# VectorE turns y in 32 by 32 blocks of channel pairs, and the queries run over 32 rows on eight tiles of TensorE

## The chip, the cores and the metric

The kernel runs on one core of one Trainium2 chip. The metric is device time in microseconds (us); the kernel before takes 170.29 us, the median of three runs (170.18 to 171.32). A core has a matrix engine, TensorE (in the profile PE, with its weight loads as PEld), and VectorE (DVE), ScalarE (ACT), GpSimd (POOL) and SyncE (SP). GpSimd and SyncE do little here but issue DMAs, each from a queue of its own. TensorE writes to PSUM, eight banks of 512 float32 columns on 128 partitions; VectorE and ScalarE take its results from there (here: drain a bank).

## What is computed

The input x is 8 batches of 4224 tokens of 192 channels. First comes a convolution over the last 7 tokens, with softmaxed taps, one set for each group of 24 channels; call its result y. Then a token mixer without softmax:

```python
wq, wk = y @ w_q, y @ w_k                    # 192 -> 64
W_tok  = scale * einsum('bsd,btd->bst', wq, wk)
mixed  = einsum('bst,btd->bsd', W_tok, y)
out    = maximum(mixed, 0.0) @ w_out         # 192 -> 192
```

Both kernels use that mixed = wq @ (scale * w_k.T @ (y.T @ y)). So per batch they make y, the Gram matrix y.T @ y (192 x 192), the small matrix M (64 x 192) from it, the queries wq, mixed = wq @ M, its relu, and the product with w_out.

## The kernel before

A batch is cut into 35 chunks of 122 tokens (128 rows of x with the 6 ahead of them). **Loads** (L513) go out from GpSimd's queue and turn float32 into bfloat16 on the way; all eight batches have room in SBUF (tile xw), 18 chunks to a DMA, 9 in the first batch. **Convolution** (L315 to L317): a band matrix of 128 by 128 for each of 8 heads times 18 chunks of 24 channels; y then stands with tokens on partitions, and one drain (L621) copies two heads. **Transposes**: the Gram matrix (L744) takes y as it stands, but the queries need channels on partitions, so TensorE transposes the first 128 channels of each chunk (L321, or L322 and L323) and the other 64 of chunks in pairs (L678), and VectorE copies both out of PSUM (ytl L648, yth L688). **Queries** (L707, L711): 64 outputs for 512 tokens on each half of the array's columns, drained at L728. **M**: a small chain after the Gram matrix (L763, L807). **Mix** (L836, L848 or L856), then relu (L873 on ScalarE, L874 on VectorE) into rt. **Product** with w_out (L902 and L920), 192 columns each, two of four token classes to a drain (L941), and a store from SyncE's queue (L949), from four buffers of out_sb. The last 128 tokens of a batch have a block of their own.

**Shapes on TensorE.** An instruction may use the whole array (128*128 in the profile), half its columns (128*64) or half its rows (64*128). Two that use different halves run side by side. The PLAN says for each step with a choice which it is: F for the whole array, P for halves.

**Order.** Nothing is decided at run time. PLAN lists 960 steps with their engine and, for TensorE, the PSUM banks; each engine's instructions follow in that order, and a step waits by semaphores for what it needs and for its banks to be drained. The second half of a batch (mix, product) is interleaved with the first half of the next.

Of the kernel before, what the change touches and what calls it, by code (L numbers as in the profile page):

```python
# [6 lines left out]
ALU = mybir.AluOpType  # L7
# [5 lines left out]

PLAN = """
1D 38G 2D 13G 37G 39G 40G 8D 19D 41G 42G 9D 56G 57G 14D 58G 59G 60G 61G 62G 63G 5D 64G 15P 65G 12D 66G 67G
68G 69G 70G 71G 72G 73G 74G 0S 22D 75G 20D 76G 77G 78G 23D 24D 25A 16P6 6D 79G 80G 21D 11D 81G 26D 27D 17P
4D 28D 18A 29D 30P5 7D 33P6 34D 35D 31A 32A 36P 84F4 85D 90F3 91A 88P1 89D 86P5 87A 116P5 142P 94P2 95D 92F1
93A 96F3 43S 98F6 99A 97D 118F4 117D 106F5 102F1 104F3 82G 100F6 143P 107D 144P 3D 105A 103A 101D 145P 83G
110F5 108F6 109A 112F3 113A 111D 119D 114F0 120F1 115A 126P2 127D 130P6 131D 47A 124F0 48A 125D 46A 44S
122F5 128P2 146P 10D 147P 121D 49A 140P4 53A 50A 132P0 123D 138P3 129D 134P2 141D 148A 149P6 52A 133A 159P4  # L20
157P0 150D 45S 51A 151F6 135A 139D 160A 155F2 158D 161F4 154A 153A 152A 222P6 136P0 162A 137A 211P1 156D
171P4 197P 54A 224A 167P2 168A 213D 165P5 172D 169P0 198P 170A 166D 221P3 210P5 163P0 199P 55A 173F2 223D
225P3 212A 217P5 164A 214P0 226P 174D 179F2 218F 180D 219D 215F 227A 177F2 178D 244F4 175F3 216A 220S 181P5
264P0 233P6 202P 176D 243P2 246A 265A 182D 228P4 232P0 245A 235D 229P 254P6 256A 201P 234A 262P2 230D 231S
185P6 186D 263A 268P4 266P0 267A 200P 255P6 269D 195P3 187P2 196A 203D 239P4 236P0 257D 258P6 240F 188A 241A
183P3 184D 204F2 205A 237F 259F 247P4 250P2 248F 251F 238A 242S 260D 261S 249A 270F0 271A 189P6 190A 304P
276P4 277A 274P0 206P6 252D 253S 272P2 305P 191P4 208A 207A 209A 328P5 275D 273A 317P0 192D 330A 288P2 289D
290P3 278P4 279D 193P5 194D 318F6 329F2 319A 286F0 340F1 280F4 320A 321P5 331A 291D 332P2 287D 342A 335P0
322P 323A 281D 333P 336P 337A 309P 292P4 284F5 334D 338S 324P2 339P0 361P6 363A 325F 293D 282F4 341A 351P6
285D 298P5 353A 326D 327S 373P0 371P2 283D 306P 374A 302P4 303A 294P6 295A 375P0 299D 372D 300P5 301D 369P2  # L30
296P4 297D 362P6 307P 376A 343P0 350P4 370A 346P2 344P 364A 385F6 347F 352A 345D 308P 310D 357P0 348A 349S
365P4 354P2 358P 386D 311F5 312D 355F 356D 359A 360S 387F6 388D 313F5 316A 315A 366F 377F0 383F2 314A 447P5
411P 425P6 378A 384D 379P0 380D 367A 368S 449A 381P3 427A 436P2 438D 412P 424P5 435P0 382A 397P3 395P4 398D
389F2 426A 428P5 396D 431P3 437A 429P 432P 458P0 390D 430A 414P 460A 457P1 459A 442P5 433D 434S 439P3 415P
440F 441A 443F 444D 445S 446P1 468P0 413P 476P3 482P5 470A 448A 399P0 393P1 416P 469P2 483A 417A 477D 400D
478F3 453P5 471A 479A 394D 450P0 418F2 419D 454F 455A 451F 480F3 391F2 409P5 452A 456S 481D 401P6 402A 464P0
461P3 465P 466A 472P6 462P 392D 403P2 410D 463D 467S 492P5 493D 488P0 489A 518P 490P3 404D 407P5 491A 484P0
408D 485D 405P2 486P3 487A 406D 520P 494P5 495D 420P1 421A 423A 506P0 504P2 502P3 422A 531P4 505D 473F 554F1
496F2 507D 543F0 474D 475S 503D 533A 497D 532F6 500F5 556A 519P 516P2 542P3 545A 534D 535P0 501D 538P5 536F
537A 517D 539F 565F2 567A 544D 546P3 549P0 547P 550P 575P2 577A 540D 541S 548D 585P5 508P2 551A 552S 564P3  # L40
586D 553P0 555A 509D 523P 587P5 588A 522P 589P0 590A 566D 521P 576P6 583P4 578A 560P2 557P0 524D 525F6 526D
561F 558F 527F6 584A 562A 498F5 530A 579P4 559D 563S 528A 571P2 568P0 572P 580P 529A 573A 569P 499D 514P5
515A 512P6 513A 570D 574S 591P2 593P0 594A 581D 582S 639P5 510P4 599P6 592D 511D 600D 638P2 640A 595P0 601P4
602D 596A 641A 625P 597P2 650P6 652A 627P 660P0 642P4 661F6 598D 607F2 605F3 606D 662A 608D 643P 644D 663A
649P0 651A 626P 609P6 645P2 656P0 653P4 610D 646P 647D 648S 657P 654P 682P6 655D 684D 630P 658A 659S 628P
694P2 695A 613P0 603P1 683P6 690P4 691A 696P2 614D 611P0 629P 685A 604D 623P1 697A 692P4 693A 672P6 612D
617P0 615P3 624D 674D 671P1 618A 664P5 686P4 631D 632F0 616D 673A 665F 666A 706F3 633D 634F0 637A 687P 688A
689S 675P1 667P5 635A 707D 678P3 676P 636A 668P 669D 670S 679P 757P0 759D 732P 677A 702P1 700P5 680A 681S
701D 746P3 748A 619P0 620D 734P 756P3 758D 703A 745P5 733P 698P0 621P2 708P3 709D 747A 704P5 699A 622A 768P4
760P0 705A 752P2 761P 762A 770D 749P5 753P 710F4 711D 750F 779F1 781D 714P0 715D 754A 736P 720P2 763P3 778P0  # L50
751A 755S 767P5 780A 721D 764P 789P2 737P 791D 769D 735P 801P0 716P2 765A 766S 730P3 797P5 738D 718P4 731D
717D 790P3 802A 739P0 719D 712P1 713D 722P2 723D 798A 792A 740A 799P5 800A 803P3 771P0 793P2 772P 773A 774P5
804D 775P 782P3 776A 777S 785P0 783P 794P 795D 796S 786P 805P5 839P 784A 726P2 809P3 806D 787A 788S 811P0
810A 727D 724P5 813P6 814D 812A 807P3 728P2 815P0 816D 808A 725A 741P1 742A 821P6 822D 825P3 826D 823P4 744A
743A 853P1 729A 864P0 866A 852P5 854A 863P2 824D 855D 840P 875P0 877A 841P 827P4 859P5 865D 867P2 856P0 868P
860P 869A 857P 828D 886P4 861D 842P 870P2 874P5 858A 862S 876A 871P 896P0 897P1 888D 843P 817P4 885P5 872D
873S 878P2 898A 899A 881P0 879P 818D 837P4 838D 844P 887A 880A 819P6 829P5 845D 846P2 847A 892P3 820D 882P
900P6 893P 830D 831P2 848P5 883A 884S 833P0 832A 851A 901P 849A 894D 889P1 850A 904P4 906A 890P 905P3 907A
834D 917P0 902D 903S 835P6 891D 895S 928P4 930A 919D 908P2 916P0 909P 910A 911S 836D 929F6 931A 912P4 918D
913P 924P0 914A 915S 920P2 925P 926A 927S 941F6 943D 921F 932P4 953P0 955D 952P6 933P 922A 923S 940P2 942A  # L60
936P0 954D 937P 956P6 957P 934D 935S 944P2 945F 948P4 949P 938A 939S 958D 959S 946A 947S 950A 951S
""".split()

COL2, ROW2, FULL = "128x64", "64x128", "128x128"


class Op:


    n = 0  # L70

    def __init__(self, engines, emit, ns, needs=(), after=(), banks=0, drains=None, vt=0.0, mode=COL2, tail=0.0, whole=False):
        self.engines = (engines,) if isinstance(engines, str) else tuple(engines)
        self.emit = emit

        self.ns = ns

        self.needs = [x for x in needs if x is not None]

        self.after = [x for x in after if x is not None]  # L80
        self.banks = banks

        self.drains = drains
        self.vt = vt
        self.mode = mode

        self.whole = whole
        self.tail = tail
        self.users = 0
        self.bank = None  # L90
        self.engine = None
        self.end = None

        self.lands = 0.0

        self.size = 0
        Op.n += 1
        self.id = Op.n


class Planner:

    ENGINES = {"P": "PE", "F": "PE", "A": "ACT", "D": "DVE", "G": "POOL", "S": "SP"}

    def __init__(self, nbank):
        self.ops = []
        self.order = []
        self.nbank = nbank
# [8 lines left out]
    def plan(self):  # L117
        drains = {}
        for op in self.ops:
            if op.drains is not None:  # L120
                drains.setdefault(op.drains.number, []).append(op)
        users = [[] for _ in range(self.nbank)]
        place = {}
        for turn in PLAN:
            number, engine, bank = re.fullmatch(r"(\d+)([PFADGS])(\d*)", turn).groups()
            op = self.ops[int(number)]
            op.engine = self.ENGINES[engine]
            if engine == "F":
                assert op.whole
                op.mode = FULL  # L130
            assert op.engine in op.engines and op.number not in place
            if op.banks:
                op.bank = int(bank)
                for i in range(op.bank, op.bank + op.banks):
                    op.needs += users[i]
                    users[i] = drains[op.number]
            assert all(x.number in place for x in op.needs + op.after)
            place[op.number] = len(self.order)
            self.order.append(op)
# [892 lines left out]
```

## Time and profile before

| what | value |
|---|---|
| time, median of three runs | 170.29 us |
| the profiled execution: span from its first to its last instruction | 168.6 us |
| TensorE busy | 158.3 us, 94% |
| ScalarE busy | 123.8 us, 73% |
| VectorE busy | 116.2 us, 69% |
| granted TensorE clock | 0.994 |
| moved by DMA | 40.31 MB |

The page gives the profiled execution by its span; the median of the runs lies 1.7 us above that, and this is taken as what lies around the span. Busy time is the time in which at least one instruction of the engine is under way. In a line of the page, L744 is the line of the kernel, then come the engine, the operation, output and inputs, for TensorE the part of the array (rows*columns), the shape, how many, the busy time and the mean in ns; behind the second bar stands the idle time ahead of it and what ended it. A timeline row has the start in us, how long the row's instructions last together, and what they are. Matmuls overlap, so how fast they follow one another is read from the starts of neighbouring rows, not from the duration of one.

### The profile page before, as it was taken

The page shows a single profiled execution, that of the slowest core. Times are in us where ns is not written, and L with a number is a line of the kernel's source. Part 1 is how long each engine was busy: PE and PEld are TensorE (multiplying, and loading weights), DVE is VectorE, ACT ScalarE, POOL GpSimd, SP SyncE. Part 2 cuts the span into 40 slices and gives each one's busy share as a digit, 9 for nine tenths or more (in the row PEclk, how much of TensorE's full clock was granted, in tenths as well). Part 3 has the DMA queues.
Part 4 walks back from the last instruction along what each step waited for, and adds up shares of the span by engine and source line. Part 5 has one row for each costly group of instructions (what it writes and reads, how often), then busy time and mean ns, then how long its engine had stood idle before and what let it go on. Part 6 is the DMA issues. An engine that isn't in the chain of part 4 may idle for free.

```text
span 168.6 us, 6398 instructions
## 1 busy us (share of the span) xinstructions
PE 158.3 (94%) x2874; PEld 116.1 (69%) x2882; DVE 116.2 (69%) x201; ACT 123.8 (73%) x207; POOL 30.3 (18%) x39
## 2 busy tenths in 40 slices
PE   6978999999999999999999999999999999999980
PEld 1458846876677886777865867787778777884640
DVE  5745878774678777566999686875957758578640
ACT  3233699798977869888566978578897889568970
POOL 7999553530503120000000000000000000000000
PEclk9999999999999999999999999999999999999997
DMA  2999999999999999999999999996644463095897
GB/s 23 172 190 185 205 191 196 189 241 301 263 328 208 300 268 276 299 251 317 284 287 199 289 282 341 235 273 232 231 176 190 189 257 149 0 368 218 315 363 283
DMA packets 48154, 40.31 MB, mean 239 GB/s; under 512 B 37632, under 2 KB 40960, under 8 KB 48128
## 3 DMA queue, kind: packets, MB, share of 16 engines
q0 software_dynamic: 36128, 13.61, 67.6%
q1 hardware_dynamic: 12000, 26.31, 43.1%
q8 instruction: 22, 0.36, 0.8%
q14 instruction: 4, 0.03, 0.1%
HBM read 27.56 MB, written 25.95 MB: 317 GB/s over the span
## 4 chain that ended last, share of the span: by engine, by line
PE 78%; ACT 8%; DMA 4%; DVE 3%; issue 2%; POOL 1%; POOLq 0%; ACTq 0%
PE ps L744 14%; PE ps L902 12%; PE ps L920 9%; PE ps L316 8%; PE ps L321 5%; PE ps L836 5%; DMA out_dram<-out_sb 4%; PE ps L678 4%; PE ps L707 4%; ACT y L621 4%; PE ps L711 3%; PE ps L856 3%; PE ps L315 3%; PE ps L322 3%; PE ps L317 2%
## 5 line engine op out<-in xcount | busy, mean ns | idle before, releaser
L621 ACT CAST y<-ps 122x864 bf16<-122x864 f32 (+3 forms) x48 | 37.2, 794 | 11.6 <-PE ps L315 5.8
L873 ACT ACTIVATE rt<-ps 128x1024 bf16<-128x1024 f32 (+3 forms) x56 | 38.7, 725 | 8.3 <-PE ps L836 6.8
L941 ACT COPY out_sb<-ps 128x768 f32<-128x768 f32 (+1 forms) x43 | 32.6, 779 | 11.9 <-PE ps L920 11.3
L513 POOL DMA_DIRECT2D xw<-in_x_dram x34 | 29.9, 909 | 29.4 <-issue 28.6
L941 DVE COPY out_sb<-ps 128x768 f32<-128x768 f32 (+1 forms) x29 | 23.9, 831 | 14.0 <-PE ps L920 12.7
L744 PEld LDWEIGHTS ps<-y 122*64 122x64 bf16 x840 | 29.4, 110 | 5.3 <-issue 2.2
L744 PE MATMUL ps<-y 122*64 122x64 bf16 (+3 forms) x840 | 32.8, 221 | 0.1
L648 DVE COPY ytl<-ps 128x976 bf16<-128x976 bf16 (+1 forms) x40 | 23.3, 592 | 7.2 <-PE ps L321 4.1
L621 DVE CAST y<-ps 122x816 bf16<-122x816 f32 (+3 forms) x24 | 21.5, 902 | 8.1 <-PE ps L317 5.4
L316 PE MATMUL ps<-xw,band 128*64 128x408 bf16 (+2 forms) x104 | 24.9, 342 | 0.0
L317 PE MATMUL ps<-xw,band 128*64 128x408 bf16 (+2 forms) x104 | 24.9, 342 | 0.0
L920 PE MATMUL ps<-wol,rt 64*128 64x192 bf16 (+1 forms) x264 | 23.9, 248 | 0.4
L902 PE MATMUL ps<-woh,rt 64*128 64x192 bf16 x264 | 22.4, 250 | 0.8 <-ACT out_sb L941 0.3
L874 DVE TENSOR_SCALAR rt<-ps 128x512 bf16<-128x512 f32 (+3 forms) x24 | 18.0, 755 | 3.1 <-PE ps L848 1.4
L920 PEld LDWEIGHTS ps<-wol,rt 64*128 64x128 bf16 (+1 forms) x264 | 15.2, 113 | 5.0 <-PE ps L902 2.5
L902 PEld LDWEIGHTS ps<-woh,rt 64*128 64x128 bf16 x264 | 11.7, 114 | 6.8 <-issue 1.8
L728 DVE CAST wqt<-ps 128x512 bf16<-128x512 f32 (+1 forms) x24 | 14.0, 583 | 2.8 <-PE ps L711 2.5
L688 DVE COPY yth<-ps 128x732 bf16<-128x732 bf16 x24 | 12.5, 534 | 4.5 <-PE ps L678 4.2
L902 PE MATMUL ps<-wol,rt 64*128 64x192 bf16 x177 | 15.4, 243 | 0.0
L711 PE MATMUL ps<-yth,wqh 128*64 128x512 bf16 (+1 forms) x72 | 14.9, 361 | 0.0
L707 PE MATMUL ps<-ytl,wql 128*64 128x512 bf16 (+1 forms) x72 | 14.5, 367 | 0.0
L321 PE MATMUL ps<-ident,y 122*128 122x122 bf16 (+1 forms) x159 | 12.0, 217 | 0.9 <-ACT y L621 0.7
(117 smaller groups left out, 209.8 us busy)
## 6 DMA issues: line engine op xcount, KB each, us to landing
out_dram<-out_sb SPq DMA_DIRECT2D x28, 768.0 KB, 7.3
xw<-in_x_dram POOLq DMA_DIRECT2D x7, 816.0 KB, 40.3
xw<-in_x_dram POOLq DMA_DIRECT2D x7, 768.0 KB, 42.9
out_dram<-out_sb SPq DMA_DIRECT2D x8, 384.0 KB, 3.1
xw<-in_x_dram POOLq DMA_DIRECT2D x2, 432.0 KB, 7.3
out_dram<-out_sb SPq DMA_DIRECT2D x8, 96.0 KB, 5.1
xw<-in_x_dram POOLq DMA_DIRECT2D x1, 384.0 KB, 5.1
xw<-in_x_dram POOLq DMA_DIRECT2D x8, 45.8 KB, 28.0
```

What stands on the lines that cost most here:

```text
L316: e.matmul(out[0:64], lhsT[:, 0:64], rhs, **k)
L317: return e.matmul(out[64:128], lhsT[:, 64:128], rhs, **k)
L321: return e.transpose(out, in_, identity)
L513: lambda e, op, part=part: e.dma_start(*part),
L621: return e.copy(dst, src) if op.engine == "ACT" else e.tensor_copy(dst, src)
L648: lambda e, op: e.tensor_copy(YTL[:, t0:t1], bank(mm_l.bank).bitcast(BF16)[:, 0:cols]),
L707: last = e.matmul(ps[64 * i : 64 * i + DH, 0:n], WQL[:, :], YTL[:, starts[i] : starts[i] + n], start=True, stop=False)
L744: mm = e.matmul(bank(GB)[p : p + 64, o : o + z - r], Y[0:w, yb, c, r : r + 64], Y[0:w, yb, c, r:z], start=st, stop=end, skip_group_check=True,
L873: return e.activation(dst, src(), AF.Relu)
L902: last = e.matmul(bank(op.bank + a)[:, (i - q) * D : (i - q) * D + D], RT[p, slot, a if lo else 2, i:n:nt], WOL[p, :] if lo else WOH[p, :] ...
L920: last = e.matmul(bank(fh.bank + a)[:, (i - q) * D : (i - q) * D + D], RT[p, slot, a, i:n:nt], WOL[p, :], start=False, stop=True, skip_gro ...
L941: return e.copy(dst, src) if op.engine == "ACT" else e.tensor_copy(dst, src)
```

## The change

Steps are also cut and named anew (each drain of two banks can be two steps, each on its own engine). What the program does afterwards:

- A batch is two runs of tokens, 18 and 17 chunks. Sixteen chunks of each make the main part; **three chunks are left** (122, 122 and 76 tokens) and go a way of their own, with their transposes on TensorE (tr_x), queries (wqx), mix (mix_x) and product (finx). The block for the last 128 tokens is gone.
- For the main part, four VectorE instructions per batch (**turn**) read y as float32 words, each a pair of bfloat16 channels, and transpose blocks of 32 by 32 words from SBUF to SBUF (tile yb). All L321 to L323 and L678 transposes of the main part and their copies (L648, L688) go.
- **Queries**: a chunk's tokens lie in four quarters on four groups of 32 partitions, each with 32 channel pairs, so a product covers 32 rows and 64 columns; six of them (three groups of pairs, two channels of a pair) add up, for four row groups and two column halves (the two runs of tokens): 48 matmuls of 512 columns, with a moving operand of stride two. They fill four banks.
- **Half-array products only**: no step has the whole-array form but the start-up ones. The last third of the product (before, L920 in either form) is always in row halves.
- **Loads** of at most 9 chunks; xw has room for 4 batches instead of 8, so a load of batch b waits for the convolution of batch b - 4. There are 48 load DMAs instead of 34. out_sb has 7 buffers instead of 4, and a store of the main part is two or three DMAs.
- **Order**: a new PLAN of 1040 steps. In GpSimd's queue the first three loads (39, 40, 41) come ahead of the step that makes the identity matrix (15); before, one load did (38, then 13).

The diff's core, with what the text above speaks of:

```diff
--- before
+++ after
 PLAN = """
-1D 38G 2D 13G 37G 39G 40G 8D 19D 41G 42G 9D 56G 57G 14D 58G 59G 60G 61G 62G 63G 5D 64G 15P 65G 12D 66G 67G
...
+0S 1D 9D 39G 17P0 13D 14D 11D 40G 4D 5D 8D 2D 24D 41G 10D 12D 25D 6D 7D 15G 3D 42G 23D 16D 21D 18P1 19P2 43G
...
+    NB = S // CW // 2
+    NA = NB + 1
+    NCC = NA + NB
+    BEGIN = (0, NB * CW)
+    LAST = 2 * NB * CW
+    NF = 4
+    NK = 16
+    COLS = (512, 512, 512, NK * 28)
+    TG = [(0, 9), (18, 9), (9, 9), (27, 8)]
+    LEFT = [(NB - 1, CW, 0), (NCC - 1, CW, CW), (NB, S - LAST, 2 * CW)]
+    NL = 2 * CW + S - LAST
+    assert NA == 18 and NB == 17 and NB == NK + 1
+    NX = 4
...
-    XW = sbuf("xw", [128, B, NCC, D], BF16)
+    XW = sbuf("xw", [128, NX, NCC, D], BF16)
-    YTL = sbuf("ytl", [128, S], BF16)
+    YB = sbuf("yb", [128, 2, 3, NCC, T], BF16)
-    NOUT = 4
+    NRL, NRH, NOUT = 4, 4, 7
...
+    def drain(make, dst, src, kind, places=(), **k):
+        def part(op, i):
+            return slice(None) if op.whole else i
+        ops = []
+        for i in range(2):
+            emit = make(lambda op, i=i: dst(part(op, i)), lambda op, i=i: src(part(op, i)))
+            op = add(both, emit, kind, writes=places, **k)
+            op.half = i
+            ops.append(op)
+        ops[0].twin, ops[1].twin = ops[1], ops[0]
...
+    AT_ONCE = 9
...
+        whole = [p for p in range(p0, p0 + n) if p not in (0, NB)]
+        for i in range(0, len(whole), AT_ONCE):
+            a, m = whole[i], len(whole[i : i + AT_ONCE])
+            at = (b * S + token(a) - KC + 1) * D
+            parts.append((XW[:, slot, a : a + m, :], bass.AP(x_t, at, [[D, 128], [CW * D, m], [1, D]]), []))
...
+    def turn(b, g):
+        tb = yb = b % 2
+        p0, n = TG[g]
+        n -= sum(p0 <= p < p0 + n for p, _, _ in LEFT)
+        def emit(e, op):
+            src = Y[:, yb, p0 : p0 + n, :].bitcast(F32).rearrange("p c (j q) -> p c j q", q=32)
+            dst = YB[:, tb, :, p0 : p0 + n, :].bitcast(F32).rearrange("p j c t -> p c j t")
+            return e.transpose(dst, src)
+        yb_place[tb][g].renew()
+        op = add("DVE", emit, "yb", writes=[yb_place[tb][g]])
...
-            for c in cs:
-                w, o = width[c], c * CW - t0
-                last = turn_halves(e, ps[:, o : o + w], Y[0:w, yb, c, 0:LO], IDENT[0:w, 0:w], op.mode)
...
+    def queries(b):
+        tb = wb = b % 2
+        def emit(e, op):
             last = None
+            for k in range(6):
+                for i in range(4):
+                    for c in range(2):
+                        q = slice(32 * i, 32 * i + 32)
+                        y = YB[q, tb, k // 2, NA * c : NA * c + NK, :].rearrange("p c t -> p (c t)")
+                        last = e.matmul(
+                            bank(op.bank, i)[rows(c), :], WQP[q, k // 2, k % 2, :], y[:, k % 2 :: 2],
+                            start=k == 0, stop=k == 5, skip_group_check=True)
+            return last
+        mm = add("PE", emit, "wq", needs=casts_q, reads=yb_place[tb], banks=4, modes="E")
...
+            def end(e, op, i0=i0, fa=fa):
                 last = None
+                for i in (i0, i0 + 1):
+                    o = (i - i0) * D
+                    for c in range(2):
+                        if op.form == 0:
+                            last = e.matmul(
+                                two(fa.bank)[0:m, c, o : o + D], RTL[rows(1 - c), lo, c, i:n:4], WOL[rows(1 - c), :],
...
+    def product_left(b):
+        xb = b % 2
+        def emit(e, op):
+            last = None
+            for k, (_, w, o) in enumerate(LEFT):
+                for src, wo in enumerate((WOL, WOZ)):
+                    for t in range(2):
+                        m = min(T, w - T * t)
                         last = e.matmul(
+                            two(op.bank)[rows(t, m), k // 2, k % 2 * D : k % 2 * D + D],
+                            RTX[:, xb, src, o + T * t : o + T * t + m], wo[:, :],
+                            start=src == 0 and k != 1, stop=src == 1, skip_group_check=True)
...
```

## The prediction

> **What bounds the kernel now.** I read the page's busy times and its chain of waits first, then the table of stretches of 8 us, then TensorE's timeline for the pace of each kind of matmul, last the groups by shape for the price of a drain.
>
> ```profile
> span 168.6 us, 6398 instructions
> ## 1 busy us (share of the span) xinstructions
> PE 158.3 (94%) x2874; PEld 116.1 (69%) x2882; DVE 116.2 (69%) x201; ACT 123.8 (73%) x207; POOL 30.3 (18%) x39
> ...
> PE 78%; ACT 8%; DMA 4%; DVE 3%; issue 2%; POOL 1%; POOLq 0%; ACTq 0%
> ```
>
> TensorE is busy for 94% of the span and makes up 78% of the chain; DMA, ScalarE and VectorE together end 15%.
>
> ```profile
> 80.00:88.00 8.00, 7.95 (x179) 6.25 (x177) 7.47 (x14) 5.27 (x10) 0.00 (x0) 1.00 1.30 291
> ...
> 96.00:104.00 8.00, 8.00 (x149) 6.06 (x149) 6.41 (x10) 6.68 (x13) 0.00 (x0) 1.00 1.24 309
> ...
> 120.00:128.00 8.00, 7.85 (x162) 6.08 (x161) 5.87 (x9) 6.58 (x9) 0.00 (x0) 1.00 0.51 199
> ```
>
> Columns: the stretch, then for PE, PEld, DVE, ACT and POOL the busy time and number of instructions, the granted clock, the DMA engines' share (two queues add up, so it passes 1) and GB/s. TensorE is full in the middle, also where VectorE is nearly full (7.47 of 8 us from 80 us). DMA is loaded until x is in (309 GB/s at 96 us), and half loaded afterwards (199 GB/s at 120 us).
>
> A busy TensorE can still hide pauses, so the pace is read from the starts:
>
> ```profile
> 79.84 0.22 PE L322 MATMUL ps<-ident,y 122*64 122x122 bf16 x1
> ...
> 80.26 0.34 PE L316 MATMUL ps<-xw,band 128*64 128x408 bf16 x1
> ...
> 80.61 0.66 PE L744 MATMUL ps<-y 122*64 122x192 bf16 x17
> 81.11 0.34 PE L316 MATMUL ps<-xw,band 128*64 128x408 bf16 x1
> ...
> 81.46 0.41 PE L707 MATMUL ps<-ytl,wql 128*64 128x512 bf16 x2
> 81.67 0.41 PE L711 MATMUL ps<-yth,wqh 128*64 128x512 bf16 x2
> ...
> 84.17 1.13 PE L678 MATMUL ps<-ident,y 122*64 122x122 bf16 x35
> 85.23 0.39 PE L836 MATMUL ps<-wqt,msb 64*128 64x512 bf16 x2
> ...
> 89.92 0.33 PE L902 MATMUL ps<-woh,rt 64*128 64x192 bf16 x4
> 90.09 0.33 PE L902 MATMUL ps<-wol,rt 64*128 64x192 bf16 x4
> ...
> 100.93 0.22 PE L322 MATMUL ps<-ident,y 122*64 122x122 bf16 x1
> ...
> 101.08 0.39 PE L836 MATMUL ps<-wqt,msb 64*128 64x512 bf16 x2
> ```
>
> Two halves side by side take together: a pair of 122 columns (0.42 us for eight pairs from 79.84) 0.0525 us; of 512 columns (81.46 to 81.67) 0.215; a pair of the 64-channel transposes 0.056 (18 pairs between 84.17 and 85.23, less one change of shape); two product pairs of 192 columns (89.92 to 90.09) 0.165, so 0.0825 each. A change of shape costs too: the last column-half pair at 100.93 is through at 100.98, and the row halves start at 101.08, so 0.10 us.
>
> By these paces a batch is 16.7 us of TensorE: convolution and Gram matrix 6720 columns each, 2.82 + 2.82; transposes 35 x 0.0525 + 18 x 0.056 = 2.84; queries 1.83 and mix 1.83; product 8 x 6 x 0.0825 + 0.25 = 4.2; M 0.36. Eight batches are 134 us. With 114 changes of shape, counted along the written order, at 0.10 (11.4), 7.8 us until the first convolution (7.84 in the chain, below) and 4.7 from the last matmul to the end (163.47 there) it makes 158. The other 10 us of the 168.6 are waits on drains, at drain engines that are 69 and 73% busy.
>
> **The change, part by part.**
>
> *TensorE, per batch.* Gone: transposes 2.84; the main queries 4 x 2 x 0.215 = 1.72; the block of 128 tokens (queries 0.11, mix 0.11, three product pairs 0.25) 0.47; 64 columns fewer in the fourth mix, 0.05. Sum 5.08. Added: main queries 6 rounds of eight tiles, each round at the pace of one 512-column pair, 1.29; for the three chunks left, transposes 0.28, queries 0.27, mix 0.27 (two passes of 320 columns each, 320/512 x 0.215 = 0.134), product 6 x 0.0825 = 0.50. Sum 2.61. Net -2.47, for eight batches **-19.8 us**. The product costs the same in row halves or whole (six passes of 192 columns), so "half arrays only" moves no work; it takes out the changes to and from the whole array but adds others: I count 124 along the new order against 114, **+1.0**.
>
> The round of eight is the unknown. The nearest rows are the warm-up, at the slower pace of the start:
>
> ```profile
> 1.26 1.89 PE L347 MATMUL ps<-runup 128*128 128x512 bf16 x4 [1.26 <-DVE runup L352]
> ...
> 4.06 1.91 PE L345 MATMUL ps<-runup 64*64 64x512 bf16 x12
> ```
>
> Four whole-array products of 512 take 1.89 us there; twelve quarter-array ones, in four rounds of 4, 4, 2 and 2 (L345's loop), take 1.91. So four tiles do run at once. Eight are not shown, nor is a moving operand of stride two. Ends: 1.29 us per batch (all eight, full stride) and 2.58 (four at a time), +10.3 us in all. I take the first, because the Gram matrix already issues a matmul every 0.028 us (three to a chunk, six chunks from 80.61 to 81.11), and eight to a round of 0.215 need 0.027. [...]
>
> *Drains.* Prices by shape:
>
> ```profile
> L941 ACT COPY out_sb<-ps 128x768 f32<-128x768 f32 x41 | 31.9, 801 | 11.7 <-PE ps L920 11.3
> ...
> L941 DVE COPY out_sb<-ps 128x768 f32<-128x768 f32 x23 | 21.9, 956 | 11.9 <-PE ps L920 10.6 <-PE ps L836 1.1
> L648 DVE COPY ytl<-ps 128x976 bf16<-128x976 bf16 x32 | 21.0, 661 | 6.7 <-PE ps L321 3.6 <-PE ps L323 3.0
> L621 ACT CAST y<-ps 122x864 bf16<-122x864 f32 x20 | 17.3, 880 | 3.1 <-PE ps L317 3.0
> ...
> L688 DVE COPY yth<-ps 128x732 bf16<-128x732 bf16 x24 | 12.5, 534 | 4.5 <-PE ps L678 4.2
> ...
> L873 ACT ACTIVATE rt<-ps 128x512 bf16<-128x512 f32 x20 | 11.5, 600 | 1.1 <-PE ps L856 0.8 <-PE ps L711 0.2
> ...
> L621 DVE CAST y<-ps 122x864 bf16<-122x864 f32 x8 | 8.3, 1050 | 1.2 <-PE ps L315 0.8 <-PE ps L317 0.4
> L874 DVE TENSOR_SCALAR rt<-ps 128x512 bf16<-128x512 f32 x12 | 8.2, 684 | 2.0 <-PE ps L848 1.4 <-PE ps L856 0.7
> ...
> L621 DVE CAST y<-ps 122x432 bf16<-122x432 f32 x6 | 3.6, 606 | 2.9 <-PE ps L317 2.2 <-PE ps L315 0.5
> ...
> L621 ACT CAST y<-ps 122x432 bf16<-122x432 f32 x6 | 2.9, 521 | 4.7 <-PE ps L315 4.3 <-PE ps L317 0.3
> ...
> L621 ACT CAST y<-ps 122x384 bf16<-122x384 f32 x3 | 1.2, 487 | 1.4 <-PE ps L315 1.4
> ...
> L621 DVE CAST y<-ps 122x384 bf16<-122x384 f32 x1 | 0.6, 559 | 1.1 <-PE ps L315 1.1
> ```
>
> ```profile
> 48.18 1.57 ACT L873 ACTIVATE rt<-ps 128x512 bf16<-128x512 f32 x3 [0.23 <-PE ps L711]
> ```
>
> Three 512-column drains in a row take 1.57 us instead of 3 x 0.600: 0.09 us of each lies over the next one, on VectorE as well I assume. Counted along the new order, ScalarE has 60 drains of 384 columns (29.2 us by 0.487), 64 of 408 to 448 (33.3 by 0.521), 52 of 512 (31.2), 12 of 768 (9.6), 19 of 816 to 1024 (16.7 by 0.880), 58 smaller (20.9 by an estimate of 0.36, under the 384 row) and 5 us of start: 146, less 275 x 0.09, so 121 us of service. VectorE loses yth (12.5) and ytl (21.0 for the 32 large ones) and gets the turns. It has 50 of 384 (28.0), 42 of 408 to 448 (25.5), 42 of 512 (28.7), 10 of 768 and more (10.3), 19 smaller (6.8), 7 us of start and 32 turns: 16 of 864 words and 16 of 672.
>
> No row shows a VectorE transpose. Nearest: 976 bfloat16 in 0.661 (0.52 ns each above the fixed part) and 864 float32 in 1.050 (1.04 ns). Ends: 0.6 us for the large ones, and two passes per word, 1.95. I take the float32 price, 1.05 and 0.85: 30.4 us, a little under what ytl and yth give back. VectorE: 137 us, less 226 x 0.09, so 117 of service.
>
> So both drain engines stand at some 120 us of service, against 140 of TensorE: neither bounds, but each is asked for more in a shorter span, since most two-bank drains are cut in two and the rest of three chunks has its own. Busy shares go from 69 and 73% to 80 to 85%, and TensorE's 10 us of waits will grow. Ends: 0, and another 10 us. I take half: **+5**.
>
> *Start.* GpSimd's queue issues two more loads ahead of the identity matrix.
>
> ```profile
> L513 POOL DMA_DIRECT2D xw<-in_x_dram x34 | 29.9, 909 | 29.4 <-issue 28.6 <-POOLq L1017 0.8
> ```
>
> ```profile
> 3.27 0.31 PE ps L322
> ...
> 7.84 1.07 PE ps L315 x4
> ...
> 109.31 7.47 DMA out_dram<-out_sb
> ...
> 163.47 0.38 PE ps L920 x4
> ```
>
> At 0.909 us each the identity comes 1.8 us later. VectorE's small chain for the taps and the first transpose (3.27, on the chain) wait for it, and behind that one in TensorE's queue stand the warm-up, the taps' products and the first convolution: **+1.8**, 0 if the x data were late anyway.
>
> *Nothing:* the 48 load issues (44 us of GpSimd, which has nothing else to do); the wait for four xw slots (batch 4 asks for the convolution of batch 0, done at some 20 us, while the queue still carries batches 1 to 3); the stores' more numerous issues from SyncE, where a late one holds those behind it, with 7 buffers for 4 as cover.
>
> Sum on the profiled execution: 168.6 - 19.8 + 1.0 + 5 + 1.8 = 156.6 us of span; with the 1.7 us between span and median, **158.3 us**.
>
> **The rivals.**
>
> *Four at a time.* The eight-tile rounds run at half pace (queue, stride two, or four banks written at once): +10.3, so 168.6, at the edge of no change. For: nothing shows eight. Against: the quarter products, and the Gram matrix's issue pace.
>
> *VectorE becomes the bound, slower.* At two passes per word the turns take 16 x (1.95 + 1.55) = 56 us instead of 30.4, and VectorE needs 143 us of service. Its first drain comes at some 10 us, with 7 us of start work done by then (3 us idle), and its last one 5 ahead of the end. At 86% in between (nearer the 93% of its fullest stretch than its 69% now) this makes 143/0.86 + 3 + 5 + 1.7 = 176 us. It decides from a mean of about 1.7 us per turn on (140 us of service). For: a reorder between partitions is unlike a copy, and four turns hold all queries of a batch. Against: ytl's fast rows show no such limit. [...]
>
> *Stores hold the span.* Both queues share the DMA engines. The chain shows one such step, 7.47 us at 109.31. With batches every 17 instead of 20 us the stores come faster while loads still run; if seven buffers don't cover it, one such stall comes on the path: 166 us. Against: only that one step now, with four buffers.
>
> **How the numbers follow.** Forecast, around 158 us: 0.50. Four at a time, 168.6: 0.14. Stores, 166: 0.12. VectorE, 176: 0.24, high, because the drain engines leave little room and a fixed order can't mend a wrong price. Range: down by the stalls not taken and cheap turns (-5, -3), 150; up to the VectorE case, 177, whose upper part is left out. 1% is about what a measurement of this kernel can tell from no change: faster 0.70 (forecast, stores and part of four at a time), same 0.06, slower 0.24.
>
> **What would show it.** In the profile after: query matmuls of 32*64 in 1.3 us per batch from first start to next kind, or 2.6; turns at 1.05 and 0.85 us; TensorE busy for 145 to 150 us; drain engines at 80 to 85%; the first convolution near 9.6 us. Wrong it would be if turns take 1.7 us on the mean, if rounds of eight take 0.4, or if the chain names ScalarE or VectorE for more than a quarter of the span.

## The result and the profile after

The changed kernel takes 217.1 us against 170.3: ratio **1.273, interval 1.267 to 1.279**. Some runs of a kernel take longer (here two of four, 224.6 and 225.2 us, at a granted clock of 0.858 and 0.883 where the others have 0.888 and 0.909), so each measured time is given as the median of the others, with "one run" beside it where only one is left. Forecast were 158.3 us, range 150 to 177. It is slower by 47 us, and by a way that the forecast priced at nothing.

The page of the profile after: span, busy times, the granted clock and the DMA engines' mean share in 40 slices, and the chain of waits by engine and by line.

```profile
span 214.2 us, 6493 instructions
## 1 busy us (share of the span) xinstructions
PE 158.1 (74%) x2788; PEld 106.0 (49%) x2788; DVE 125.0 (58%) x226; ACT 126.4 (59%) x276; POOL 40.0 (19%) x53
...
PEclk9999589999988999999975999969999999997555
DMA  5999999999999999998621456159519736868462
...
PE 51%; DMA 18%; ACT 7%; SPq 4%; another core or an unknown queue 3%; DVE 3%; issue 3%; POOL 1%; DVEq 0%; POOLq 0%
DMA out_dram<-out_sb 12%; PE ps L898 10%; PE ps L714 9%; PE ps L646 8%; PE ps L794 6%; PE ps L913 5%; PE ps L976 4%; DMA xw<-in_x_dram 4%; SPq L586 3%; PE ps L836 3%; PE ps L857 3%; DMA wkx<-in_moe_w_k_dram 3%; ACT wqt L379 2%; ACT y L379 2%
```

TensorE is as long busy as before (158.1 us), but this is 74% of the span and not 94. The chain, once 78% TensorE, holds 18% of DMA, most of it stores of `out_sb`. The last four slices have DMA work at 0.8, 0.4, 0.6 and 0.2 and nothing of TensorE.

The stretches that were shown of before, one more at 104 us, and the last 22 us (columns as there):

```profile
80.00:88.00 8.00, 8.00 (x154) 4.96 (x155) 7.33 (x14) 5.32 (x12) 0.00 (x0) 1.00 1.38 258
96.00:104.00 8.00, 6.71 (x130) 4.76 (x124) 3.17 (x6) 4.16 (x9) 0.00 (x0) 1.00 0.87 261
104.00:112.00 8.00, 2.31 (x28) 1.72 (x27) 0.56 (x1) 1.15 (x5) 0.00 (x0) 0.89 0.36 106
120.00:128.00 8.00, 7.96 (x139) 5.15 (x137) 7.58 (x14) 6.57 (x14) 0.00 (x0) 1.00 0.52 131
192.00:200.00 8.00, 0.00 (x0) 0.00 (x0) 0.08 (x1) 0.00 (x0) 0.00 (x0) 0.73 0.82 252
200.00:208.00 8.00, 0.00 (x0) 0.00 (x0) 0.00 (x0) 0.00 (x0) 0.00 (x0) 0.50 0.42 114
208.00:214.20 6.20, 0.00 (x0) 0.00 (x0) 0.00 (x0) 0.00 (x0) 0.00 (x0) 0.50 0.40 128
```

At 80 and 120 us TensorE is as full as before. Between them, at 104 us, it does 2.31 us in 8, and the drain engines stand too. The last matmul ends at 191.2 us, 23 us ahead of the end, where before had 4.8. In the last 14 us the DMA engines' mean share is 0.40 to 0.42: some 6.5 of 16 at work, while stores are all there is to do; from 200 to 204 us it is 0.18, some 3 of 16.

What holds the stretch at 104 us is in the chain (start, length, what), in the waits of 95 to 115 us (sum, number, longest), and in SyncE's queue of issues (start, length, what):

```profile
97.11 15.54 DMA out_dram<-out_sb
...
112.68 0.57 DVE out_sb L379
...
113.30 2.79 PE ps L794 x41
```

```profile
DVE out_sb L379 <- DMA out_dram<-out_sb: 10.1, 2, 7.5
ACT out_sb L379 <- DMA out_dram<-out_sb: 8.5, 2, 7.5
...
PE ps L794 <- DVE out_sb L379: 7.0, 1, 7.0
```

```profile
105.22 0.25 SPq L997 DMA_DIRECT2D out_dram<-outx  x1
105.52 10.18 SPq L998 DMA_DIRECT2D out_dram<-outx  x1
115.80 4.14 SPq L958 DMA_DIRECT2D out_dram<-out_sb  x3
```

One step of the chain is a store that lands 15.5 us after its issue; before, the 768 KB ones took 7.3 in the median. Drains wait up to 7.5 us for its buffer, TensorE's queries 7.0 us for a drain, and after the pause they run in 2.79 us at a granted clock of 0.50, where those from 86.11 us take 1.57 at 1.00. In the meantime SyncE *issues one DMA for 10.18 us*: L998, the 76 leftover rows of a batch (57 KB). All stores stand behind it in the queue. Added over the trace, SyncE spends 126.7 us on issuing 96 stores (18.4 on 44 before), 43.8 of them on the eight issues of L998, median 4.23 us.

The loads are late too. The last x load, issued at 72.0 us, lands at 152.6 us, and between 136 and 153 us TensorE's convolution waits for two such loads (sum, number, longest); before has no wait of this kind:

```profile
PE ps L646 <- DMA xw<-in_x_dram: 6.5, 2, 3.5
```

### The profile page after: what moved, and what is told of

Same layout as the page of the kernel before. It is cut to its first block, busy times and chain, and to the rows that moved or that the text cites. A ratio compares the mean times of both kernels' runs of the same rounds, so it can differ in the third digit from the quotient of the medians.

```text
span 214.2 us, 6493 instructions
## 1 busy us (share of the span) xinstructions
PE 158.1 (74%) x2788; PEld 106.0 (49%) x2788; DVE 125.0 (58%) x226; ACT 126.4 (59%) x276; POOL 40.0 (19%) x53
## 4 chain that ended last, share of the span: by engine, by line
PE 51%; DMA 18%; ACT 7%; SPq 4%; another core or an unknown queue 3%; DVE 3%; issue 3%; POOL 1%; DVEq 0%; POOLq 0%
DMA out_dram<-out_sb 12%; PE ps L898 10%; PE ps L714 9%; PE ps L646 8%; PE ps L794 6%; PE ps L913 5%; PE ps L976 4%; DMA xw<-in_x_dram 4%; SPq L586 3%; PE ps L836 3%; PE ps L857 3%; DMA wkx<-in_moe_w_k_dram 3%; ACT wqt L379 2%; ACT y L379 2%
## 5 line engine op out<-in xcount | busy, mean ns | idle before, releaser
L563 POOL DMA_DIRECT2D xw<-in_x_dram x48 | 39.5, 850 | 32.5 <-PE ps L646 30.2
L379 ACT COPY out_sb<-ps 128x384 f32<-128x384 f32 (+3 forms) x65 | 33.0, 545 | 20.0 <-DMA out_dram<-out_sb 10.4
L379 ACT CAST y<-ps 128x432 bf16<-128x432 f32 (+4 forms) x67 | 37.2, 598 | 9.9 <-PE ps L646 9.3
L379 DVE COPY out_sb<-ps 128x384 f32<-128x384 f32 (+3 forms) x48 | 26.5, 574 | 25.5 <-PE ps L913 12.5
L714 PE MATMUL ps<-y 122*64 122x64 bf16 (+4 forms) x840 | 35.0, 225 | 3.8 <-issue 2.4
L646 PE MATMUL ps<-xw,band 128*64 128x408 bf16 (+3 forms) x288 | 32.8, 340 | 6.7 <-DMA xw<-in_x_dram 6.5
L714 PEld LDWEIGHTS ps<-y 122*64 122x64 bf16 (+1 forms) x840 | 31.2, 113 | 6.9 <-issue 2.1
L676 DVE STREAM_TRANSPOSE yb<-y 128x864 f32<-128x864 f32 (+1 forms) x32 | 30.0, 960 | 2.9 <-ACT y L379 2.6
L379 DVE CAST y<-ps 128x432 bf16<-128x432 f32 (+4 forms) x42 | 25.0, 626 | 7.1 <-PE ps L646 6.9
L646 PEld LDWEIGHTS ps<-xw,band 128*64 128x64 bf16 x288 | 15.2, 116 | 14.5 <-DMA xw<-in_x_dram 7.0
L898 PE MATMUL ps<-wol,rtl 64*128 64x192 bf16 (+1 forms) x256 | 22.3, 252 | 0.0
L913 PE MATMUL ps<-wol,rtl 64*128 64x192 bf16 (+1 forms) x256 | 21.7, 264 | 0.1
L913 PEld LDWEIGHTS ps<-wol,rtl 64*128 64x128 bf16 (+1 forms) x256 | 13.0, 136 | 4.6 <-PE ps L898 2.2
L898 PEld LDWEIGHTS ps<-wol,rtl 64*128 64x128 bf16 (+1 forms) x256 | 14.7, 133 | 0.0
```

The lines of the kernel that those rows point to most:

```text
L379: return e.copy(dst(op), src(op)) if op.engine == "ACT" else e.tensor_copy(dst(op), src(op))
L563: "POOL", lambda e, op, dst=dst, src=src: e.dma_start(dst, src), "load", dma=(name, sem, 16), needs=needs
L646: last = e.matmul(y[rows(c), :], BAND[:, h, T * c : T * c + T], xs, start=True, stop=True, skip_group_check=True)
L676: return e.transpose(dst, src)
L714: last = e.matmul(bank(g)[rows(k), o : o + z - a], y[:, a : a + T], y[:, a:z], start=p == 0 and a == o, stop=p == NCC - 1, skip_group_chec ...
L898: last = e.matmul(two(op.bank)[0:m, c, o : o + D], RTL[rows(c), lo, c, i:n:4] if own else RTH[rows(c), hi, i:n:4], WOL[rows(c), :] if own ...
```

## The experiments

**Theory F (few engines).** A store would be dealt out over only so many of the 16 DMA engines as divide its rows, and some of the changed kernel's stores have 122, 76 and 6 rows as their outer dimension where before had 128. The few engines would fall behind, and the queue behind them. **Theory N (number):** more stores, more issue time on SyncE. **Theory D:** drains and the written order hold TensorE, the stores only follow.

A first sign of F lies in the two traces already: the semaphore updates recorded for a store, counted per store.

```
store (outer rows)          updates per store
before, all: 128                16
after, blocks 0-2: 16           16
after, block 3: 6 (of 16)        7
after, leftovers: 122 and 76     8 for the two (3 + 5)
```

The stores of the runs below go the same way: 16 updates for 112, 64 and 16 rows, 13 for 12, 11 for 10, 5 for 124 and for 4. Each count is the largest divisor of the rows up to 16, and one more where that is under 16. I read this as one update from each engine and one more for the rest of the 16, so 16, 6, 2 and 4 engines in the table; where engines of a store are counted below, it is by this reading, as no view names them. A second sign is the share: from 202 to 204 us of the profile after, the packets of SyncE's stores are the 768-byte rows of the leftovers alone, and the DMA engines' mean share is 0.18, some 3 of 16.

**Leftover stores cut.**

```diff
-  OUTX[0:122, xb, 0:2, :]           OUTX[0:76, xb, 2, :]
+  rows 0:112 and 112:122            rows 0:64 and 64:76
```

> The two leftover stores of each batch cut by rows: 122 rows into 112 and 10, 76 rows into 64 and 12. Same bytes, same order, 16 more stores in the kernel. Theory F (few engines): a store is dealt out over only as many of the 16 DMA engines as divide its rows, so 122 rows go to 2 engines and 76 to 4; these engines are late and everything behind them waits. Then 94 KB per batch leave the two busiest engines; with 22.5 GB/s of one engine (before's last 8.6 us: 324 GB/s at a DMA share of 0.90, over 16) that is 8 x 94 / 22.5 = 33 us of service: 221 falls to 185 to 200, and the issue of the leftover stores (3 to 10 us now) to under 1 us each. Theory N (number of stores: SyncE's queue is late by their count): 16 more issues, 221 to 235. Theory D (the written order and the drains hold TensorE, the stores only follow): 218 to 224.

Measured: 192.4 us (one run; the others 196.7 to 198.0, the median of all four 197.1), 19 to 25 us less with 16 stores *more*; the updates per batch went from 8 to 56 (16 + 11 + 16 + 13), the issues of the 76 rows from 4.23 to 0.51 and 0.55 us. Inside F's range; N and D had no gain.

**The fourth block's stores cut.**

```diff
-  parts = [(0, [[4 * D, 6], [CW * D, NK]], 0, c, n) for c in range(2)]
+  parts = [(16 * g, [[CW * D, NK]], 4 * g, c, n) for c in range(2) for g in range(6)]
```

> The stores of each batch's fourth block, 96 partitions as 6 rows of 16 in the output, cut into six of 16 partitions; the leftover stores stay. Same bytes and order, 80 to 100 more stores. Theory F: six engines took 590 KB of a batch, 98 KB each, and now 16 take 37 KB each: 61 KB less on the busiest, 8 x 61 / 22.5 = 22 us: 195 to 208, with the leftover stores' issues still 2 us and more. Theory N: nearly twice the stores, 235 to 270. Theory D: 218 to 224.

Measured: 216.9 us, no gain. F said 195 to 208 and missed; D, with no change, comes nearest. The leftovers' issue still takes 4.31 us in the median, and 186 stores take 145 us of issue. That a gain by F and a loss by N cancel here is not shown by this run.

**Both cuts,** by the two diffs above.

> Both cuts at once. Theory F: 55 us of service leave the busiest engines, more than the 50 us by which the kernel is over its own work, so what is left is the work and the late start: 163 to 175; the end comes back to about 5 us behind the last matmul (22.6 now), and no drain waits over 3 us for a store. Theory N: 240 and more. Theory D: 218 to 224.

Measured: 207.6 us; F's 163 to 175 is far off. The drains hardly wait for stores any more (1.2 us at most, 7.5 uncut), but 30.2 us of end follow the last matmul, and SyncE now issues 202 stores in 115 us. With the weights moved as well:

**Both cuts, weights earlier.**

```diff
-  needs=x_place[0][1].writers        load order q, out, k
+  needs=x_place[0][0].writers        load order q, k, out
```

> Both cuts, and the weight loads wait for the first two of the x loads alone, not for the third (the groups of the second quarter), with the key weights issued ahead of the output weights. If the late weights hold the start (queries of batch 0 at 25 us, mixes at 31, where before had mixes at 24): 5 to 7 us less than with both cuts alone, 158 to 168. If the start's loss is hidden by something later: within 1.5 us of it.

Measured: 200.5 us (one run; the others 204.0 to 206.0), so 7.1 us less by that run and 1.6 to 3.6 by the others: whether the 5 to 7 expected came is not settled, and the 158 to 168 did not. In the trace of the run with 200.5 us, SyncE's queue at the end is:

```profile
154.18 25.70 SPq L958 DMA_DIRECT2D out_dram<-out_sb  x40
...
182.17 14.38 SPq L958 DMA_DIRECT2D out_dram<-out_sb  x29
```

The last matmul ends at 168.3 us, 7.2 us earlier than with both cuts alone; 40 issues in 25.7 us and 29 in 14.4, one behind the other at 0.5 to 0.6 us each, make the other 30 us. So N is right too, as a second price. To tell the two apart, the kernel before was given the first fault without the second, and the other way round.

**Before, one store of each batch in 124 and 4 rows; the same in 112 and 16.**

```diff
-  dma_start(dst, src)                                       # 128 partitions, block 1
+  for p, z in ((0, 124), (124, 128)): dma_start(dst[p:z], src[p:z])    # or (0, 112), (112, 128)
```

> The kernel before, with one of each batch's four 768 KB stores cut by partitions into 124 and 4, so that by theory F 744 KB of it lie on 4 engines, 186 KB each where an even share is 48. 8 more stores. Theory F: engines 0 to 3 then have 203 + 138 KB of stores and 203 KB of loads a batch, 544 KB at 22.5 GB/s = 24 us against the 20 us of a batch: 180 to 200, and the issue of the 124-row store, 0.37 us uncut, takes several us. Theory N (only the number and issue time of stores matters, dealt out evenly): 170 to 172.

> The same store of the kernel before cut into 112 and 16 partitions: as many stores and bytes as with 124 and 4, but both pieces on 16 engines. Theory F: 170 to 172. Theory N: the same as with 124 and 4.

Measured: **211.2 us** (ratio 1.240, 1.231 to 1.250) and **171.4** (1.005, 1.003 to 1.008). Same bytes, same number of stores, one number apart. The two pieces have 5 updates each with 124 and 4 rows, and 16 each with 112 and 16. Steps over 7 us in the chains, first with 124 and 4 rows, then with 112 and 16:

```profile
41.53 13.32 DMA out_dram<-out_sb
...
58.78 14.65 DMA out_dram<-out_sb
...
88.31 14.44 DMA out_dram<-out_sb
...
140.69 11.79 DMA out_dram<-out_sb
...
177.39 12.47 DMA out_dram<-out_sb
```

```profile
108.57 7.87 DMA out_dram<-out_sb
```

F alone brings in late stores and a loss like the one after the change, and more of it than the 10 to 30 us that I had worked out: the chain has DMA for 32% of the span, since not only do four engines carry more by F, the drains also wait for the buffers behind them (28.5 us in eleven waits). One part of the expectation missed: the pieces of 124 rows (744 KB) are issued in 0.28 us in the median and not in several. Long issues are not needed for the loss, and 5 updates in place of 16 do not alone make an issue long.

**Before, every store cut in four.**

```diff
-  dma_start(dst, src)
+  for p in range(0, 128, 32): dma_start(dst[p : p + 32], src[p : p + 32])
```

> The kernel before with each store cut by partitions into four of 32 rows, all on 16 engines: 176 stores for 44, 60 to 75 us of issue on SyncE for 18. If the number of stores and their issue time alone make a kernel late: 185 and more. If only stores on few engines do: 170 to 174.

Measured: 181.6 us (1.065, 1.060 to 1.070), between the two. Its issues take 97 us, 0.55 each. The last matmul comes 2.1 us later than in before (165.9 for 163.8), and 14.6 us of end follow it, for 4.8:

```profile
99.82 78.76 SPq L950 DMA_DIRECT2D out_dram<-out_sb  x105
```

Number costs mostly at the end, where the queue that has grown must run out.

**Without the stores of batches 0 to 6.**

```diff
+  op.left_out = b < B - 1            # store and storex: no instruction, no wait
```

> The changed kernel with all stores of batches 0 to 6 left out (those outputs are missing), the last batch's kept; the rest and its order as they are. If stores and the late start are all that the prediction missed: 158.3 plus the start's 7 us: 162 to 168. If TensorE's own stages or the drains were mis-sized too, as the two cut kernels' last matmuls at about 169 to 173 us suggest: 170 to 180. If neither the stores nor their issue hold it (theory D): above 200.

Measured: 187.2 us, above the two ranges that I had thought likely and under D's. The windows tell why:

```profile
128.00:160.00 32.00, 31.50 (x648) 23.88 (x648) 23.89 (x41) 25.88 (x58) 0.00 (x0) 1.00 0.01 3
...
170.00:186.00 16.00, 0.00 (x0) 0.00 (x0) 0.51 (x2) 0.34 (x1) 0.00 (x0) 0.62 0.47 138
```

The work ends at 169.7 us, as the cut kernels showed; 15 us of end follow, made by the last batch's 19 stores alone, which are halved, and of which block 3 and the leftovers still lie, by F, on 2, 4 and 6 engines. The late x loads are gone too: the last one lands at 81.0 us where it was 152.6.

**Half of the stores on GpSimd's queue.**

```diff
+  op.on = "POOL" if b >= 3 and (j in (1, 3) or leftover)     # with the leftovers cut, weights earlier
```

> The changed kernel with the leftover stores cut to 112, 10, 64 and 12 rows, the weights waiting for the first x loads alone, the key weights ahead, and from batch 3 on half of the stores (blocks 1 and 3 and the leftovers) issued by GpSimd's queue, which has no loads left from 81 us on. If SyncE's issuing is what is late (90 us of issue in 112 stores with the leftovers cut, against 18 in 44 before): the tail of 22 us behind the last matmul goes, 168 to 178. If the DMA engines themselves are late whatever queue feeds them: 188 to 198.

Measured: 190.6 us (one run; the others 193.6 to 197.7), as if the queue did not matter. Block 3 stayed a store of 6 rows there, so this does not separate the engines from the queue, and I draw nothing from it.

**Fourth block as 16 rows with no store more.** The 96 partitions are brought into the order 16 by 6 where the queries are drained:

```diff
-  WQT[...].rearrange("p (q k t) -> p k q t")                        # one copy, 7 groups of 4
+  WQT[0:384] as "(k q t)", WQT[384:448] as "(k t)"                  # two copies
-  [[4 * D, 6], [CW * D, NK]]
+  [[CW * D, NK], [4 * D, 6]]
```

> The leftover stores cut as in the kernel with 197 us, and the fourth block's queries drained in another order (two copies instead of one), so that its 96 output partitions lie as 16 rows of 6 and not as 6 rows of 16: same bytes, same addresses, same number of stores, but by theory F 16 engines instead of 6, 61 KB a batch less on the busiest, 22 us: 174 to 186. Theory N (issue time on SyncE alone): no store fewer, 192 to 198.

Measured: **185.5 us** (1.087, 1.081 to 1.093), inside F's range; 16 updates for each of these stores. It is now *faster than the kernel without the stores of seven batches*, and its last matmul, 172.1 us, is 2.4 us behind that one's: the stores now hold the work by little more than that. Of the 58.8 us between forecast and result this settles **31.6**.

**What is left: start and leftover product.**

```profile
16.00:20.00 4.00, 1.31 (x40) 1.09 (x33) 0.58 (x2) 0.06 (x1) 4.00 (x6) 0.95 1.43 210
20.00:24.00 4.00, 1.52 (x32) 1.55 (x33) 1.32 (x4) 1.96 (x6) 4.00 (x6) 0.50 1.52 190
24.00:28.00 4.00, 3.23 (x59) 1.29 (x55) 1.46 (x4) 0.80 (x3) 0.42 (x1) 0.50 1.60 193
```

```profile
2.86 7.78 DMA xw<-in_x_dram
...
18.73 5.38 DMA wkx<-in_moe_w_k_dram
...
25.28 2.79 PE ps L794 x41
```

TensorE stands 5.9 us between 16 and 28 us (the 6.5 of an expectation below is too high), at a clock that falls to 0.50, and the first queries take 2.79 us. The chain says: the weights wait for an x load (10.65 us), fourteen issues follow, the last lands at 24.1. The leftover product, from the kernel without stores:

```profile
113.92 0.25 PE L979 MATMUL ps<-wol,rtx 128*64 128x192 bf16 x1
...
114.17 0.29 PE L979 MATMUL ps<-woz,rtx 128*64 128x192 bf16 x2
114.25 0.42 PE L979 MATMUL ps<-wol,rtx 128*64 128x192 bf16 x2
114.60 0.45 PE L979 MATMUL ps<-woz,rtx 128*64 128x192 bf16 x2
114.98 0.32 PE L823 MATMUL ps<-ytx,wql 128*64 128x320 bf16 x1
```

The first eight matmuls, of 64 and 58 columns, take 0.33 us, from 113.92 to 114.25. The last four, two of them 12 columns wide, take 0.73, to 114.98: the narrow ones stand in the trace of the profile after as 128*12, the others as 128*64 and 128*58. With the narrow ones as a shape of their own (58 taken as 64) it has 153 changes of shape, where I had counted 124; with all three as one, as when padded to 64 columns, it has 124.

```diff
-  m = min(T, w - T * t)
+  m = T if k == 2 else min(T, w - T * t)      # 52 more columns drained before it
```

> The changed kernel without the stores of batches 0 to 6, as the one with 187.2 us (those outputs are missing), with two more edits. The weights wait for the first x loads only and the key weights go ahead: batch 0's queries came 2.3 us earlier so (22.84 against 25.12 us). And the leftover product's last half is made 64 columns wide instead of 12 (padded): its four matmuls stood alone for 0.18 us each, 0.73 a batch where two pairs take 0.16, so 8 x 0.55 = 4.4 us. If both are on the path: 179 to 182. If waits for drains take their place: 184 to 187.

Measured: 180.4 us, 6.8 less, as expected if both are on the path.

**All edits; weights waiting for no x load.** The first and the third have all edits that gained so far, and the last batch's second halves on ScalarE's queue; the second has the stores of the kernel with 185.5 us and the weights alone.

```diff
+  op.on = "ACT" if i0 else None        # stores; first and third
-  needs=x_place[0][0].writers
+  needs=[]                             # weights; second and third
```

> The changed kernel with all that the runs point to: leftover stores cut, the fourth block's rows in the order for 16 engines, weights early, the leftover product padded, and the last batch's second halves issued by ScalarE's queue beside SyncE's. Without stores the last matmul was at 171 us; 2.3 less for the start and 4.4 for the padding give 164, and 6 to 10 for the end: 170 to 176. If the stores still hold buffers and drains: 180 to 190.

> The changed kernel with all stores on 16 engines (185.45 us), the weight loads waiting for no x load and the key weights ahead. In that kernel TensorE stands 6.5 us between 16 and 28 us, and the first eight-tile queries then run at a granted clock of 0.50 (2.79 us for 1.49). If the late weights make this stall: batch 0's queries start near 18 us instead of 25.3 and the whole is 177 to 180. If the weights only push the first x loads back by as much, or a later wait takes its place: 183 to 187.

> The kernel with all five edits (180.2 us), its weights too waiting for no x load (there they waited for the first two). By the stall that is left there between 16 and 24 us, 3.9 us of TensorE: 174 to 177. With no gain: 179 to 181. That it comes under the kernel before (170.5) neither theory expects: its work after the start and its end of 8.7 us remain.

Measured: 180.2 (170 to 176 was expected, and 180 to 190 if the stores still hold buffers and drains: the second came), 181.0 (177 to 180: missed by 1.0) and **176.2 us** (174 to 177: met; all four runs 175.9 to 178.7). With no wait for x the first queries come at 20.8 us and take 1.54:

```profile
5.08 9.46 DMA xw<-in_x_dram
...
20.77 1.54 PE ps L794 x42
```

The last matmul comes 5.5 us earlier, and the time falls by 4.5: the late weights were the stall, but the x load issued at 5.08 us, now beside them, lands at 14.5 us and not at 12.9, so that part of it stays. The best kernel of all is still 3 to 5% slower than before.

## Why the prediction was wrong

*The step that failed* stands under "Nothing": "the stores' more numerous issues from SyncE, where a late one holds those behind it, with 7 buffers for 4 as cover". It measured 31.6 us. I had seen the queue and the number, and gave both to the buffers; of the stores' shape I looked at bytes alone. 122, 76 and 6 rows for 128 put 183, 57 and 576 KB of each batch into stores of 3, 5 and 7 updates, by F on 2, 4 and 6 engines. Seven buffers were no cover: the drains of the two engines waited for stores six times, 22.2 us in all. Nor did the loads stay free of it: 6.5 us of waits, with the last one landing at 152.6 us, and at 81.0 without the stores of seven batches. None of the three signs by which the forecast was to be known as wrong showed, since none was about stores.

*The rival "stores hold the span"* had the right mechanism, a chance of 0.12 and a price of one 7.47 us stall. It was priced from a kernel in which every store has 16 updates, and so could not show it. The slower rival, VectorE, did not come in.

*Turns:* right. Priced at 1.05 and 0.85 us:

```profile
L676 DVE STREAM_TRANSPOSE yb<-y 128x864 f32<-128x864 f32 x16 | 17.2, 1072 | 2.6 <-ACT y L379 2.2
L676 DVE STREAM_TRANSPOSE yb<-y 128x672 f32<-128x672 f32 x16 | 13.6, 848 | 0.4 <-ACT y L379 0.4
```

*Eight tiles at once:* nearly. 48 matmuls were to take 1.29 us:

```profile
86.11 1.57 PE L794 MATMUL ps<-yb,wqp 32*64 32x512 bf16 x48
```

The six batches at a granted clock of 1.00 take 1.49 to 1.57, 0.25 to 0.26 a round, so +1.6 us or a little more in all. In batch 0, at 24.95 us, and at 113.30, behind the pause, the rounds take 2.79 us, near half that pace; the granted clock is 0.50 there.

*Leftover product:* 0.50 a batch, measured 1.06, +4.5 us, by the two 12-column pieces. I had taken them as halves.

*Start:* the first convolution at 9.6, measured 9.62: right, but the loss lay behind it. Fourteen weight loads in place of nine, behind an x load, cost 4.5 us by the run without the wait (in which the key weights also go ahead).

*End:* 4.7 us were kept from before. It is 23.0 in the changed kernel, 12.4 with the leftovers cut and the fourth block as 16 rows: the last batch's stores, halved, are a queue of their own.

*Drain engines:* 80 to 85% busy was forecast; in no version of the changed kernel do they pass 72%. TensorE busy for 145 to 150 us came true only with all edits, 149.2 and in the last kernel 147.1:

```profile
span 174.0 us, 6517 instructions
## 1 busy us (share of the span) xinstructions
PE 147.1 (85%) x2788; PEld 99.9 (57%) x2788; DVE 124.4 (72%) x227; ACT 125.9 (72%) x283; POOL 40.0 (23%) x53
...
PE 61%; ACT 14%; DMA 6%; issue 5%; DVE 5%; ACTq 3%; POOL 2%; POOLq 0%
```

```profile
0.00:32.00 32.00, 23.34 (x406) 14.27 (x408) 21.25 (x57) 18.73 (x47) 28.18 (x39) 1.00 1.38 170
...
80.00:128.00 48.00, 42.21 (x774) 28.14 (x770) 32.64 (x54) 36.09 (x79) 0.00 (x0) 1.00 1.09 242
```

*What stays open.* Its span is 174.0 for the 156.6 of the sum. The end has 3.4 us of the difference (8.1 for 4.7). TensorE's idle time up to the last matmul has 6.5 (18.8, where 5.5 of before and 6.8 added were forecast): 8.7 us lie ahead of 32 us, and 5.8 between 80 and 128 us, where before has 0.9. Of these 5.8, 3.3 are three pauses of about 1 us (at 89.4, 97.9 and 106.7 us) for which the profile shows nothing that TensorE waited for. The kernel without stores has none of the three and stands for 1.1 us in that stretch; by what way stores could bring them about was not tested.

The other 7.6 are busy time: it fell by 11.2 us and not by 18.8. If each busy instant is given to the matmul that started last, products rose by 6.0 us and mixes by 4.3, where 2.0 and 0.9 were forecast, and the Gram matrix and the convolution by 2.9, where nothing was; transposes fell by 2.6 more than forecast. Why these are slower was not tested.

Two readings ahead of the sum were off as well. Of the 10 us of before that it calls waits on drains, TensorE stands for 5.5 at most, so the rest was work that no row had priced. And 18 pairs in 1.06 us, less 0.10 for the change of shape, are 0.053 us each and not 0.056, which is 0.4 us in all.

## What to carry over

Before a tile's rows are regrouped, look at what the new rows make of the stores: here, stores whose outer dimension had 2, 4 or 6 as its largest divisor up to 16 (122, 76 and 6 rows) made 3, 5 and 7 updates in place of 16, and the queue, the buffers and the loads behind them paid for it, with 31.6 us. Cut such a store at a multiple of 16 (112 and 16 rows: 171.4 us; 124 and 4: 211.2), or bring the order of partitions to 16 rows by n, ahead of cutting it into many: each store more cost about half a microsecond of SyncE here, and that comes due at the end. And price stores by issues and shape, not by bytes; an idle queue in the old profile says nothing about new shapes.

## What was not expected of the hardware

One issue can be dear: a store of 57 KB with 5 updates held SyncE for 4.23 us in the median and 10.18 at most, the same rows as 64 and 12 for 0.51 and 0.55. Why is not shown. It always stands behind the 122 rows with 3 updates, while the 124 rows with 5 in the other kernel were issued in 0.28 us.

Late landings alone are enough for the loss, in a kernel that has none of the change: 124 and 4 rows in place of 112 and 16, in one store of each batch, took it from 171.4 to 211.2 us.

Issues of stores with 16 updates differ by shape: in the median 0.37 us for 128 partitions of 2 rows (768 KB) before, and after the change 0.85 for 16 by 8 (384 KB) and 1.12 for 16 by 2 (48 KB), so that a small store can be as dear as a large one.
